# First attention batch: query scaling folded in, 64x64 turns, and work moved from VectorE to ScalarE and GpSimd

## The chip, the core and the metric

One core of a Trainium2 chip runs the whole program. Its engines are TensorE (PE, with its weight loads as PEld), VectorE (DVE), ScalarE (ACT), GpSimd (POOL) and SyncE (SP), which issues most of the DMA transfers; ScalarE's queue issues a few more at the start. The metric is the device time of one execution in microseconds, lower is better.

## The reference

A thresholded attention over 8 batches of 8 heads (576 rows, 64 columns a head), and then a bilinear feed-forward layer (FFN) over its 4608 x 512 output:

```python
scale = 1.0 / np.sqrt(q.shape[-1])
scores = scale * np.matmul(q, k.transpose(0, 1, 3, 2))
thresh = np.max(scores, axis=-1, keepdims=True) - tau
scores = np.where(scores >= thresh, scores, -1000000000.0)
scores = scores - np.max(scores, axis=-1, keepdims=True)
attn = np.exp(scores)
attn = attn / (np.sum(attn, axis=-1, keepdims=True) + 1e-09)
attn_out = np.matmul(attn, v)
# (B, H, S, D) -> x of (B*S, H*D)
a = x @ w_a
b = x @ w_b
return a * b @ w_out
```

The three weight matrices (512 x 1536 twice, 1536 x 512) arrive as 8-byte floats and are turned into 4-byte ones in the kernel, by operations on the integer halves.

## The kernel before

Two heads make a pair, four pairs (HP = 4) a batch. A *unit* (i, u) is 128 query rows of both heads of pair i. The first batch has 18 units, in the order (0,0), (1,0), (2,0), (3,0), (0,1), ... One pass of the main loop is a *slot* g: it works on several units at once, each at its own step. All instructions keep the order in which they are written, engine by engine (`keep_order`), so what stands ahead on an engine's queue runs first.

For its unit, slot g does:

- `scores` (L398 to L413): on TensorE the scores of both heads into two banks of the four in PSUM (L404); on VectorE each row's maximum (L411) and the threshold, maximum minus `cut` (L412).
- `weigh` (L423): on ScalarE, for each head, the bias (maximum times minus the scale, L431) and the exponential of scaled scores plus bias (L432); on VectorE the masked weights with their row sums (L435).
- `reciprocal` (L446, L448) on VectorE.
- For the first eight units (`BY_PE` = 8) `diagonals` (L456): ScalarE scales the identity by each head's reciprocals (L462). One slot later `turn_pe` (L469) transposes and normalises the weights in one: each of 9 column blocks of 64 is the stationary operand of a matmul with a head's diagonal (L479), 18 matmuls with 128 rows, 64 columns and 128 moving columns. ScalarE copies two banks of the result (L481), VectorE the ninth block (L482).
- Two slots later `weighted_unit` (L587) multiplies by the values (L542). `settle` (L546) copies the product out of PSUM: one half on ScalarE (L549), the other in two 64 x 64 pieces on VectorE (L550). GpSimd exchanges halves (L565).

Units from the ninth on are transposed by VectorE (L498) and by DMA through DRAM (`turn_blocks`, `turn_back`) instead.

Between these steps the weights are converted: 36 pieces of 0.5 MB, two or three a slot. A piece takes two passes on ScalarE (L298, L299), a clamp (L305) and an integer add (L324) on GpSimd, and two passes on VectorE (L311, L319). SP issues the loads of the pieces (L271); each is made to wait for the TensorE instruction that stands just before it in the program, and for the buffer that it fills. FFN matmuls of the first rows (L824, `pab`) start in slot 5, and fill TensorE between the attention steps. From about 130 us on TensorE goes through FFN and attention without a pause.

Ahead of the loop, ScalarE's queue issues the keys of pair 0 (L198) and then `tau` (L339); VectorE copies the transposed queries of pair 0 (L383) and then computes the scalars (L1042 to L1047): whether tau is at least 0, the scale and its negative, and `cut`.

Of the kernel before, what the change touches and what calls it, by code (L numbers as in the profile page):

```python
# [13 lines left out]
AF = mybir.ActivationFunctionType  # L14
ALU = mybir.AluOpType
AX = mybir.AxisListType
# [38 lines left out]
def kernel(  # L55
# [38 lines left out]
    nc = tc.nc  # L94
    B, H, S, D = q.shape
    P = 128
# [3 lines left out]
    HP = H // 2  # L100
    NT = 4
# [148 lines left out]
    first_sb = first_u32.bitcast(FP32)  # L250
# [77 lines left out]
    scalars = const.tile([P, 8], FP32, name="scalars")  # L328
    tau_sb = scalars[:, 5:6]
# [4 lines left out]
        rooms.append(t.rearrange("p n e -> p (n e)")[0:R, 0:ROWS])  # L334
    rooms += [sums_sb[0:R, c:c + ROWS] for c in range(0, 5 * ROWS, ROWS)]
    rooms = [t.rearrange("p (n w) -> p n w", n=NR) for t in rooms]
    load_rows(0, "q", rooms[0])
    load_rows(0, "k", rooms[1], nc.scalar)
    nc.scalar.dma_start(tau_sb, tau.to_broadcast([P, 1]))  # L339
    load_rows(1, "q", rooms[2])  # L340
    load_rows(1, "k", rooms[3], nc.scalar)
    load_weights(2)
# [5 lines left out]
    load_rows(3, "k", rooms[7])  # L348
    ident = more_sb[:, 2 * QUARTER:2 * QUARTER + P]
    make_identity(nc, ident)  # L350

# [4 lines left out]
    x_of, xtail_of = {}, {}  # L356
# [11 lines left out]
    def prep_pe(i, name):  # L368

        m = loaded[i][name]  # L370
        if name == "q":
            mT = first_sb[:, i * S:(i + 1) * S]
        else:
            mT = work.tile([P, S], FP32, tag="kT", bufs=HP, name="kT")
        tp = banks(SH, "tp")
        for c in range(2):
            for n in range(NR // 2):
                nc.tensor.transpose(tp[:, c, n * R:(n + 1) * R], m[:, c * (NR // 2) + n], ident[0:R, 0:R])
        prepared.setdefault(i, {})[name] = mT
        return mT, tp  # L380

    def prep_copy(mT, tp):
        nc.vector.tensor_copy(mT.rearrange("p (c k) -> p c k", c=2), tp)  # L383

    def columns():

# [2 lines left out]
    def scores(i, u):  # L389
        qT, kT = prepared[i]["q" if i < HP else "q1" if u > 1 else "q0"], prepared[i]["k"]  # L390
        base = HALF if i >= HP and u > 1 else 0
        sc = [banks(SH, "sc") for _ in range(2)]
        wide = D if u == NT else columns()
        each = [(c, t, j) for c in range(2) for t in range(2 if wide == D else 1) for j in range(2)]
        if units.index((i, u)) < BY_HEAD:
            each.sort(key=lambda x: x[2])
        for c, t, j in each:
            r = slice(j * D, (j + 1) * D)  # L398
            if u < NT:
                m, o, q0 = j, t, u * P + t * D - base  # L400
            else:
                m, o, q0 = t, j ^ t, MAIN - base
                qT, kT = prepared[i + t]["q" if i < HP else "q1"], prepared[i + t]["k"]
            nc.tensor.matmul(sc[m][o * D:o * D + wide, c], qT[r, q0:q0 + wide],  # L404
                             kT[r, c * SH:(c + 1) * SH], start=True, stop=True)
        mx = small.tile([P, 2], FP32, tag="mx", name="mx")
        thr = small.tile([P, 2], FP32, tag="thr", name="thr")
        bias = small.tile([P, 2], FP32, tag="bias", name="bias")
        for j in range(2):
            c = slice(j, j + 1)  # L410
            nc.vector.tensor_reduce(mx[:, c], sc[j], axis=AX.XY, op=ALU.max)  # L411
        nc.vector.tensor_scalar(thr, mx, cut, None, op0=ALU.subtract)  # L412
        scored[i, u] = (sc, thr, bias, mx)  # L413

    def rooms_of(i, u):
# [6 lines left out]
    def weigh(i, u):  # L422

        sc, thr, bias, mx = scored.pop((i, u))
        n = len(sc)
        sums = small.tile([P, 2], FP32, tag="sums", name="sums")
        ws = rooms_of(i, u)
        sb = [s.rearrange("p c (n e) -> p c n e", e=Q) for s in sc]
        wb = [w.rearrange("p (c n) e -> p c n e", c=2) for w in ws]
        for j in range(n):  # L430
            nc.scalar.activation(bias[:, j:j + 1], mx[:, j:j + 1], AF.Copy, scale=e_nscale)  # L431
            nc.scalar.activation(wb[j], sb[j], AF.Exp, bias=bias[:, j:j + 1], scale=e_scale)  # L432
# [23 lines left out]
    def diagonals(i, u):  # L456

        ws, rcp = weights[i, u]
        g = units.index((i, u))
        dg = first_sb[:, HP * S + g % 3 * 2 * P:HP * S + (g % 3 + 1) * 2 * P].rearrange("p (j q) -> p j q", j=2)  # L460
        for j in range(2):
            nc.scalar.activation(dg[:, j], ident, AF.Copy, scale=rcp[:, j:j + 1])  # L462
        weights[i, u] = (ws, dg)

    def turned_tile():
# [2 lines left out]
    def turn_pe(i, u):  # L468

        ws, dg = weights.pop((i, u))  # L470
        ws = [w.rearrange("p n e -> p (n e)") for w in ws]
        wT = turned_tile()[:, 0:G].rearrange("p g s e -> p (g s e)").rearrange("p (s w) -> p s w", w=P)
        turned[i, u, "pe"] = [wT[:, :, y * D:(y + 1) * D] for y in range(2)]
        tp = banks(512, "tp").rearrange("p y (s q) -> p y s q", s=NT)
        last = banks(P, "tp")
        for s in range(NSLOT):
            for j, w in enumerate(ws):
                to = (last[:, 0] if s == 2 * NT else tp[:, s // NT, s % NT])[j * D:(j + 1) * D]
                nc.tensor.matmul(to, w[:, s * D:(s + 1) * D], dg[:, j], start=True, stop=True)  # L479
        for y in range(2):  # L480
            nc.scalar.copy(wT[:, y * NT:(y + 1) * NT], tp[:, y])  # L481
        nc.vector.tensor_copy(wT[:, 2 * NT], last[:, 0])  # L482

    def parts(i, u):

# [57 lines left out]
                                     start=(s == 0), stop=(s == NSLOT - 1))  # L543
        return pv

    def settle(out, pv, c0, c1, others):  # L546

        n = c1 - c0
        one = [nc.scalar.copy(out[:, 0:n], pv[:, 0, c0:c1])]  # L549
        two = [nc.vector.tensor_copy(out[c * D:(c + 1) * D, n:2 * n], pv[(1 - c) * D:(2 - c) * D, 1, c0:c1])  # L550
               for c in range(2)]
# [38 lines left out]
    def weighted_unit(i, u):  # L590

        b, hp = pairs[i]
        wT = turned.pop((i, u, "pe"))
        pv = product([lambda rows, s, t=t: t[rows, s] for t in wT], loaded[i]["v"], P)
        settled_of[i] = settled_of.get(i, 0) + P
        if (b, 0) not in x_of:
            x_of[b, 0] = x_tile("xT")
            state["xs"] = x_tile("xS")
        settle(x_of[b, 0][:, hp, u * P:(u + 1) * P], pv, 0, D, ([], []))
        exchange(x_of[b, 0], state["xs"], hp, u * P, (u + 1) * P, nc.gpsimd)  # L600
        if hp == HP - 1:
# [436 lines left out]
    prep_copy(*prep_pe(0, "q"))  # L1038
    kT, tp = prep_pe(0, "k")
    nc.scalar.copy(kT.rearrange("p (c k) -> p c k", c=2), tp)  # L1040
    ok, e_scale, e_nscale, cut, big = (scalars[:, c:c + 1] for c in range(5))
    nc.vector.tensor_scalar(ok, tau_sb, 0.0, None, op0=ALU.is_ge)  # L1042
    nc.vector.tensor_scalar(e_scale, ok, SCALE, None, op0=ALU.mult)
    nc.vector.tensor_scalar(e_nscale, ok, -SCALE, None, op0=ALU.mult)
    nc.vector.tensor_scalar(big, ok, -BIG, BIG, op0=ALU.mult, op1=ALU.add)
    nc.vector.tensor_scalar(cut, tau_sb, 0.0, INV_SCALE, op0=ALU.max, op1=ALU.mult)
    nc.vector.tensor_tensor(cut, cut, big, op=ALU.add)  # L1047
    early = {}

    def convert_rest(g, k):  # L1050
# [6 lines left out]
    n = 0  # L1057
# [4 lines left out]
    for g in range(len(units) + PV_LAG):  # L1062
# [9 lines left out]
        if BY_PE + 1 < g <= len(units) + 1:  # L1072
            n = g - PV_LAG
# [3 lines left out]
        if here:  # L1077
            i, u = units[g]
# [9 lines left out]
            weighted_unit(*units[g - 2])  # L1088
            running["owed"] -= NSLOT * P // 2
        if g < 3:  # L1090
            prep_copy(*prep_pe(g + 1, "q"))
        convert_rest(g, 0)
        if g == 0:
            for c in range(0, 2 * QUARTER - 2 * CW + 1, 2 * CW):
# [131 lines left out]
```

## Time and profile before

| what | us |
|---|---|
| median of 3 timed runs | 1420.72 (1419.43 to 1420.96) |
| span of the profiled execution, first to last instruction | 1417.0 |
| TensorE busy in it | 1370.2 |
| VectorE / ScalarE / GpSimd busy | 1013.7 / 679.9 / 495.7 |
| TensorE idle before 130 us | 30.1 |
| VectorE busy between 76 and 110.3 us | 33.75 of 34.30 |
| TensorE idle from 130 to 1380 us | 10.3 |
| DMA rate, 24 to 76 us | 229 GB/s |

The profile is of one execution; its answers give that execution's span and no time from outside, so the table sets the span beside the timed runs: their median is 3.7 us more. "Busy" is the union of an engine's instructions; a line such as `PE 1370.2 (97%) x33836` gives busy time, its share of the span and the number of instructions. In the timeline a line gives start, duration, engine, source line, operation, output and input, shapes, a count, and in brackets the idle time of the engine before it with what ended it. "issue" there is a wait for nothing that the profile shows.

### The profile page before, as it was taken

How to read it: one execution, taken by the hardware profiler on the slowest of the kernel's cores; microseconds unless marked ns; L12 is line 12 of the kernel's file. 1: busy time of each engine (PE TensorE's matmuls, PEld its weight loads, DVE VectorE, ACT ScalarE, POOL GpSimd, SP SyncE). 2: the span in 40 equal slices, each digit the busy share in tenths (PEclk: the TensorE clock that was granted, in tenths of full speed). 3: DMA queues.
4: the chain of work that ended last, by engine and by line, in shares of the span. 5: the costliest groups of instructions: out<-in, count | busy, mean ns of one | idle time of the engine just before them, and what ended most of it. 6: DMA issues, size and time to landing. Idle time of an engine off the chain costs nothing.

```text
span 1417.0 us, 76257 instructions
## 1 busy us (share of the span) xinstructions
PE 1370.2 (97%) x33836; PEld 1229.6 (87%) x33836; DVE 1013.7 (72%) x2200; ACT 679.9 (48%) x1245; POOL 495.7 (35%) x678
## 2 busy tenths in 40 slices
PE   6788999999999999999999999999999999999998
PEld 5677579989878887979998999999888899799997
DVE  6898986778777877776767777677777776744424
ACT  5786554545445454545444545454545455431110
POOL 2674541606060606042333324150606060608100
PEclk9999999999999999999999999999999999999999
DMA  9967776667756775666555675567655775550000
GB/s 212 235 193 219 182 214 163 178 153 183 198 135 173 198 188 155 178 156 184 142 134 149 168 193 158 144 160 199 168 144 152 191 201 154 135 152 18 4 19 18
DMA packets 327000, 223.20 MB, mean 158 GB/s; under 512 B 171536, under 2 KB 310800, under 8 KB 326672
## 3 DMA queue, kind: packets, MB, share of 16 engines
q1 hardware_dynamic: 323712, 216.95, 59.2%
q8 instruction: 266, 4.36, 1.3%
q10 hardware_dynamic: 2960, 1.38, 0.4%
q14 instruction: 62, 0.51, 0.1%
HBM read 128.58 MB, written 89.65 MB: 154 GB/s over the span
## 4 chain that ended last, share of the span: by engine, by line
PE 86%; DVE 7%; DMA 3%; issue 2%; SPq 1%; ACT 0%; POOL 0%; DVEq 0%; POOLq 0%; ACTq 0%
PE pab L720 29%; PE po L885 20%; PE pab L824 16%; PE pv L542 10%; PE sc L404 10%; DVE mx L411 2%; DVE tw L498 2%; SPq L144 1%; DMA wT<-swap 1%; DVE tw L435 1%; PE tp L479 1%; DMA raw<-in_moe_w_a_dram 1%; DMA raw<-in_moe_w_b_dram 1%; DVE thr L412 0%; DVE u L790 0%
## 5 line engine op out<-in xcount | busy, mean ns | idle before, releaser
L411 DVE TENSOR_REDUCE mx<-sc 128x1 f32<-128x576 f32 x288 | 204.7, 752 | 125.8 <-PE sc L404 125.4
L454 ACT ACTIVATE tw<-tw,rcp 128x576 f32<-128x576 f32 x272 | 196.5, 770 | 202.3 <-DVE rcp L448 202.3
L682 POOL TENSOR_TENSOR h<-h,u 128x512 f32<-128x512 f32 x28 | 35.2, 1276 | 601.0 <-DVE h L794 426.1
L432 ACT ACTIVATE tw<-sc,bias,scalars 128x576 f32<-128x576 f32 x288 | 239.8, 833 | 10.9 <-PE pab L720 0.4
L435 DVE SCALAR_TENSOR_TENSOR tw<-sc,thr,tw 128x576 f32<-128x576 f32 x288 | 221.5, 799 | 10.4 <-ACT tw L432 9.9
L885 PE MATMUL po<-wo_sb,h 64*64 64x256 f32 x3264 | 205.8, 376 | 1.2 <-DVE h L794 1.1
L498 DVE STREAM_TRANSPOSE tw<-tw 128x576 f32<-128x576 f32 x272 | 194.4, 752 | 0.8 <-ACT tw L454 0.8
L885 PEld LDWEIGHTS po<-wo_sb,h 64*64 64x64 f32 x3264 | 157.0, 133 | 25.7 <-DVE h L794 2.6
L542 PE MATMUL pv<-wT,vm 64*64 64x160 f32 (+3 forms) x5184 | 169.2, 275 | 7.6 <-issue 3.6
L542 PEld LDWEIGHTS pv<-wT,vm 64*64 64x64 f32 x5184 | 157.4, 136 | 19.1 <-issue 9.8
L404 PE MATMUL sc<-kT,qT 64*64 64x288 f32 x2016 | 168.0, 404 | 1.1 <-DVE xt L550 0.5
L853 POOL TENSOR_TENSOR h<-h 128x256 f32<-128x256 f32 x168 | 117.4, 732 | 107.4 <-PE po L885 97.2
L885 PE MATMUL po<-sums_u,h 64*64 64x256 f32 x2448 | 153.4, 376 | 0.7 <-DVE h L832 0.7
L720 PE MATMUL pab<-xU,wb_sb 64*64 64x128 f32 x4352 | 138.0, 269 | 0.4 <-issue 0.3
L720 PEld LDWEIGHTS pab<-xU,wb_sb 64*64 64x64 f32 x4352 | 132.2, 133 | 3.7 <-issue 1.1
L885 PEld LDWEIGHTS po<-sums_u,h 64*64 64x64 f32 x2448 | 117.6, 133 | 19.4 <-DVE h L832 1.3
L404 PEld LDWEIGHTS sc<-kT,qT 64*64 64x64 f32 x2016 | 101.8, 133 | 22.6 <-issue 5.0
L549 ACT COPY xT<-pv 128x128 f32<-128x128 f32 (+1 forms) x68 | 17.7, 260 | 201.8 <-PE pv L542 200.2
L431 ACT ACTIVATE bias<-mx,scalars 128x1 f32<-128x1 f32 x288 | 83.1, 288 | 64.0 <-DVE mx L411 63.7
L550 DVE COPY xT<-pv 64x128 f32<-64x128 f32 (+1 forms) x136 | 38.1, 280 | 91.0 <-PE pv L542 89.7
L720 PE MATMUL pab<-xS,wa_sb 64*64 64x128 f32 x2176 | 101.8, 269 | 0.1
L531 ACT COPY kept<-po 128x512 f32<-128x512 f32 x65 | 34.8, 536 | 123.0 <-PE po L885 113.9
(156 smaller groups left out, 2414.3 us busy)
## 6 DMA issues: line engine op xcount, KB each, us to landing
wT<-swap SPq DMA_DIRECT2D x244, 288.0 KB, 3.9
swap<-tw SPq DMA_DIRECT2D x480, 144.0 KB, 2.9
vm<-in_v_dram SPq DMA_DIRECT2D x128, 72.0 KB, 2.5
swap<-tw SPq DMA_DIRECT2D x128, 72.0 KB, 3.0
kT<-in_k_dram SPq DMA_DIRECT2D x112, 72.0 KB, 3.3
wT<-swap SPq DMA_DIRECT2D x56, 144.0 KB, 3.3
out_dram<-kept SPq DMA_DIRECT2D x28, 256.0 KB, 3.9
qT<-in_q_dram SPq DMA_DIRECT2D x112, 40.0 KB, 2.8
```

The source lines that it names most:

```text
L404: nc.tensor.matmul(sc[m][o * D:o * D + wide, c], qT[r, q0:q0 + wide], kT[r, c * SH:(c + 1) * SH], start=True, stop=True)
L411: nc.vector.tensor_reduce(mx[:, c], sc[j], axis=AX.XY, op=ALU.max)
L431: nc.scalar.activation(bias[:, j:j + 1], mx[:, j:j + 1], AF.Copy, scale=e_nscale)
L432: nc.scalar.activation(wb[j], sb[j], AF.Exp, bias=bias[:, j:j + 1], scale=e_scale)
L435: nc.vector.scalar_tensor_tensor(out=wv, in0=sb[j], scalar=thr[:, j:j + 1], in1=wv, op0=ALU.is_ge, op1=ALU.mult, accum_out=sums[:, j:j + 1])
L454: nc.scalar.activation(w, w, AF.Copy, scale=rcp[:, j:j + 1])
L498: nc.vector.transpose(w, w)
L542: nc.tensor.matmul(pv[c * D:(c + 1) * D, y], vm[rows, s], wT[y](rows, s), start=(s == 0), stop=(s == NSLOT - 1))
L720: nc.tensor.matmul(out[c * D:(c + 1) * D, r, f * P:(f + 1) * P], w[g][k][rows, w0:w0 + D], moving[k][rows], start=(fresh and k == 0 and f ...
L824: nc.tensor.matmul(pab[c:c + columns(), r], w[rows, f // n, k, fs + c:fs + c + columns()], moving, start=(k == 0), stop=(k == H - 1))
L853: (nc.vector if state["over"] else nc.gpsimd).tensor_tensor(*a, **kw)
L885: nc.tensor.matmul(po[c * D:(c + 1) * D, r, y], ht[rows, t0:t0 + D], other[rows, f], start=(f == 0), stop=(f == NF // 2 - 1))
```

## The change

In the first batch (i < HP):

- the transposed queries are multiplied by the scale when they are copied out of PSUM (`prep_copy` with `e_scale`), so that the scores are scaled already; the scalars stand ahead of that copy, and the load of tau ahead of the keys of pair 0 on ScalarE's queue;
- the maxima are taken with their sign turned, and serve as the bias of the exponential; the bias instructions go;
- the threshold is taken on ScalarE, between the two exponentials: minus the negated maximum, plus a new scalar `ncut_first`.

In the first eight units:

- the diagonals are 64 columns for each row half (a 128 x 64 tile `twice`, two identities on top of each other, times the reciprocals), made by one GpSimd instruction for both heads;
- `turn_pe` does each block in four matmuls of 64 rows, 64 columns and 64 moving columns: 36 instead of 18;
- the ninth block and all of the product are copied by ScalarE.

```diff
+    nc.scalar.dma_start(tau_sb, tau.to_broadcast([P, 1]))
     load_rows(0, "q", rooms[0])
     load_rows(0, "k", rooms[1], nc.scalar)
-    nc.scalar.dma_start(tau_sb, tau.to_broadcast([P, 1]))
...
+    twice = first_sb[:, HP * S + 3 * P:HP * S + 3 * P + D]
+    nc.gpsimd.tensor_tensor(twice, ident[:, 0:D], ident[:, D:P], op=ALU.add)
...
+    def prep_copy(mT, tp, scale=None):
+        out = mT.rearrange("p (c k) -> p c k", c=2)
+        if scale is None:
+            nc.vector.tensor_copy(out, tp)
+        else:
+            nc.vector.tensor_scalar(out, tp, scale, None, op0=ALU.mult)
...
-            nc.vector.tensor_reduce(mx[:, c], sc[j], axis=AX.XY, op=ALU.max)
-        nc.vector.tensor_scalar(thr, mx, cut, None, op0=ALU.subtract)
+            nc.vector.tensor_reduce(mx[:, c], sc[j], axis=AX.XY, op=ALU.max, negate=i < HP)
+        if i >= HP:
+            nc.vector.tensor_scalar(thr, mx, cut, None, op0=ALU.subtract)
...
+            if i < HP:
+                nc.scalar.activation(wb[j], sb[j], AF.Exp, bias=mx[:, j:j + 1])
+                if j == 0:
+                    nc.scalar.activation(thr, mx, AF.Identity, bias=ncut_first, scale=-1.0)
+            else:
...
-        for j in range(2):
-            nc.scalar.activation(dg[:, j], ident, AF.Copy, scale=rcp[:, j:j + 1])
+        nc.gpsimd.tensor_tensor(dg, twice.unsqueeze(1).to_broadcast([P, 2, D]), rcp.unsqueeze(2).to_broadcast([P, 2, D]), op=ALU.mult)
...
         for s in range(NSLOT):
-            for j, w in enumerate(ws):
-                to = (last[:, 0] if s == 2 * NT else tp[:, s // NT, s % NT])[j * D:(j + 1) * D]
-                nc.tensor.matmul(to, w[:, s * D:(s + 1) * D], dg[:, j], start=True, stop=True)
-        for y in range(2):
-            nc.scalar.copy(wT[:, y * NT:(y + 1) * NT], tp[:, y])
-        nc.vector.tensor_copy(wT[:, 2 * NT], last[:, 0])
+            for r in range(2):
+                rows = slice(r * D, (r + 1) * D)
+                for j, w in enumerate(ws):
+                    to = (last[:, r] if s == 2 * NT else tp[:, r, s])[j * D:(j + 1) * D]
+                    nc.tensor.matmul(to, w[rows, s * D:(s + 1) * D], dg[rows, j], start=True, stop=True)
+        for r in range(2):
+            nc.scalar.copy(wT[:, 0:2 * NT, r * D:(r + 1) * D], tp[:, r])
+        nc.scalar.copy(wT[:, 2 * NT].rearrange("p (r q) -> p r q", r=2), last)
...
-        settle(x_of[b, 0][:, hp, u * P:(u + 1) * P], pv, 0, D, ([], []))
+        settle(x_of[b, 0][:, hp, u * P:(u + 1) * P], pv, 0, D, ([], []), nc.scalar.copy)
...
+    nc.vector.tensor_scalar(ncut_first, tau_sb, 0.0, -1.0, op0=ALU.max, op1=ALU.mult)
     nc.vector.tensor_tensor(cut, cut, big, op=ALU.add)
+    nc.vector.tensor_tensor(ncut_first, ncut_first, big, op=ALU.subtract)
+    prep_copy(*prep_pe(0, "q"), e_scale)
```

More of the change, by code (lines that the diff above doesn't have):

```diff
@@ L380, in prep_pe @@
         return mT, tp
-    def prep_copy(mT, tp):
-        nc.vector.tensor_copy(mT.rearrange("p (c k) -> p c k", c=2), tp)
+    def prep_copy(mT, tp, scale=None):
[4 more added lines that the diff above has]
+            nc.vector.tensor_scalar(out, tp, scale, None, op0=ALU.mult)
     def columns():
@@ L430, in weigh @@
         for j in range(n):
-            nc.scalar.activation(bias[:, j:j + 1], mx[:, j:j + 1], AF.Copy, scale=e_nscale)
-            nc.scalar.activation(wb[j], sb[j], AF.Exp, bias=bias[:, j:j + 1], scale=e_scale)
+            if i < HP:
[3 more added lines that the diff above has]
+            else:
+                nc.scalar.activation(bias[:, j:j + 1], mx[:, j:j + 1], AF.Copy, scale=e_nscale)
+                nc.scalar.activation(wb[j], sb[j], AF.Exp, bias=bias[:, j:j + 1], scale=e_scale)
         for j in range(n):
@@ L459, in diagonals @@
         g = units.index((i, u))
-        dg = first_sb[:, HP * S + g % 3 * 2 * P:HP * S + (g % 3 + 1) * 2 * P].rearrange("p (j q) -> p j q", j=2)
-        for j in range(2):
-            nc.scalar.activation(dg[:, j], ident, AF.Copy, scale=rcp[:, j:j + 1])
+        dg = first_sb[:, HP * S + g % 3 * P:HP * S + (g % 3 + 1) * P].rearrange("p (j q) -> p j q", j=2)
+        nc.gpsimd.tensor_tensor(dg, twice.unsqueeze(1).to_broadcast([P, 2, D]), rcp.unsqueeze(2).to_broadcast([P, 2, D]), op=ALU.mult)
         weights[i, u] = (ws, dg)
@@ L473, in turn_pe @@
         turned[i, u, "pe"] = [wT[:, :, y * D:(y + 1) * D] for y in range(2)]
-        tp = banks(512, "tp").rearrange("p y (s q) -> p y s q", s=NT)
-        last = banks(P, "tp")
+        tp = banks(512, "tp").rearrange("p y (s q) -> p y s q", q=D)
+        last = banks(D, "tp")
         for s in range(NSLOT):
-            for j, w in enumerate(ws):
-                to = (last[:, 0] if s == 2 * NT else tp[:, s // NT, s % NT])[j * D:(j + 1) * D]
-                nc.tensor.matmul(to, w[:, s * D:(s + 1) * D], dg[:, j], start=True, stop=True)
-        for y in range(2):
-            nc.scalar.copy(wT[:, y * NT:(y + 1) * NT], tp[:, y])
-        nc.vector.tensor_copy(wT[:, 2 * NT], last[:, 0])
+            for r in range(2):
[6 more added lines that the diff above has]
+        nc.scalar.copy(wT[:, 2 * NT].rearrange("p (r q) -> p r q", r=2), last)
     def parts(i, u):
@@ L544, in product, with settle @@
         return pv
-    def settle(out, pv, c0, c1, others):
+    def settle(out, pv, c0, c1, others, engine=None):
         n = c1 - c0
         one = [nc.scalar.copy(out[:, 0:n], pv[:, 0, c0:c1])]
-        two = [nc.vector.tensor_copy(out[c * D:(c + 1) * D, n:2 * n], pv[(1 - c) * D:(2 - c) * D, 1, c0:c1])
-               for c in range(2)]
+        copy = engine or nc.vector.tensor_copy
+        two = [copy(out[c * D:(c + 1) * D, n:2 * n], pv[(1 - c) * D:(2 - c) * D, 1, c0:c1]) for c in range(2)]
         for mine, theirs in ((one, others[1] + two), (two, others[0] + one)):
@@ L1036 @@
     second = {i: g for g, (i, u) in enumerate(units) if u == 2}
-    prep_copy(*prep_pe(0, "q"))
-    kT, tp = prep_pe(0, "k")
-    nc.scalar.copy(kT.rearrange("p (c k) -> p c k", c=2), tp)
     ok, e_scale, e_nscale, cut, big = (scalars[:, c:c + 1] for c in range(5))
+    ncut_first = scalars[:, 6:7]
     nc.vector.tensor_scalar(ok, tau_sb, 0.0, None, op0=ALU.is_ge)
@@ L1046 @@
     nc.vector.tensor_scalar(cut, tau_sb, 0.0, INV_SCALE, op0=ALU.max, op1=ALU.mult)
+    nc.vector.tensor_scalar(ncut_first, tau_sb, 0.0, -1.0, op0=ALU.max, op1=ALU.mult)
     nc.vector.tensor_tensor(cut, cut, big, op=ALU.add)
+    nc.vector.tensor_tensor(ncut_first, ncut_first, big, op=ALU.subtract)
+    prep_copy(*prep_pe(0, "q"), e_scale)
+    kT, tp = prep_pe(0, "k")
+    nc.scalar.copy(kT.rearrange("p (c k) -> p c k", c=2), tp)
     early = {}
@@ L1090 @@
         if g < 3:
-            prep_copy(*prep_pe(g + 1, "q"))
+            prep_copy(*prep_pe(g + 1, "q"), e_scale)
         convert_rest(g, 0)
```

## The prediction

> **What bounds the kernel now.** First the engine totals of the page, then a table of busy time by stage (columns: window in us, its length, then busy us and instruction count of TensorE, weight loads, VectorE, ScalarE and GpSimd, the granted clock, the DMA share, GB/s):
>
> ```profile
> PE 1370.2 (97%) x33836; PEld 1229.6 (87%) x33836; DVE 1013.7 (72%) x2200; ACT 679.9 (48%) x1245; POOL 495.7 (35%) x678
> ```
> ```profile
> 24.10:47.30 23.20, 18.45 (x384) 14.75 (x384) 21.82 (x53) 19.26 (x42) 14.19 (x19) 1.00 1.13 229
> 47.30:76.00 28.70, 23.76 (x457) 21.45 (x457) 23.60 (x53) 21.96 (x47) 20.14 (x24) 0.88 0.97 229
> 76.00:110.30 34.30, 27.56 (x514) 24.36 (x510) 33.75 (x66) 28.78 (x57) 24.97 (x27) 1.00 0.74 205
> ...
> 130.00:1380.00 1250.00, 1239.74 (x31316) 1114.13 (x31316) 889.12 (x1928) 584.46 (x1054) 423.78 (x591) 1.00 0.59 155
> ```
>
> From 130 us on TensorE is busy 1239.7 of 1250 us in an order that the change leaves alone. So the time changes by what the start-up before 130 us gains or loses, and that passes through whole. There are three stages in it. From 24 to 47 us VectorE is busy 94%, DMA is full. From 76 to 110 us VectorE is busy 33.75 of 34.30 us: it is the limit. Between them, from 47 to 76, no engine is, and the timeline shows why (start, us, engine, line, operation, count, idle before it):
>
> ```profile
> 33.20 1.28 PE L542 MATMUL pv<-wT,vm 64*64 64x64 f32 x72
> ...
> 34.41 2.19 PE L479 MATMUL tp<-first_u,tw 128*64 128x128 f32 x36
> ...
> 47.29 1.88 PE L542 MATMUL pv<-wT,vm 64*64 64x64 f32 x59 [0.56 <-issue]
> ...
> 54.66 1.16 PE L824 MATMUL pab<-xT,wb_sb 64*128 64x128 f32 x16 [0.56 <-issue]
> ...
> 62.58 0.54 PE L479 MATMUL tp<-first_u,tw 128*64 128x128 f32 x5 [1.13 <-issue]
> ...
> 70.09 0.34 PE L542 MATMUL pv<-wT,vm 64*64 64x64 f32 x6 [1.83 <-issue]
> ```
>
> TensorE stops four times in the middle of a run of like matmuls, waiting for no semaphore ("issue"). Counting its instructions in the trace (a weight load and a matmul each count one, a semaphore wait one), the holds stand before numbers 961, 1217, 1473 and 1729: 256 apart. The DMA view of a window between two of them names the cause:
>
> ```profile
> q1 hardware_dynamic: 196, 0.35, 101.0%
> q8 instruction: 1, 0.02, 5.1%
> issues: line engine op xcount, KB each, median us to landing
> more_u<-in_moe_w_b_dram SPq DMA_DIRECT2D x2, 256.0 KB, 8.8
> ```
>
> One 16,384-byte packet on the instruction queue at 51.86, among weight loads that fill the engines. Such packets start at 28.36, 36.25, 44.45, 51.86, 59.84, 67.31 and 71.96 us and take 1.3 us; each hold ends 1.46 to 1.57 us after one ends, and under full DMA the next starts 4.6 to 5.2 us after a hold ends. So I read it as code brought one block of 256 ahead, queued behind weight data: from 39.35 (entry to the block at 705) the blocks begin 7.94, 7.36, 7.93 and 7.51 us apart. TensorE gets 256 instructions per 7.7 us there, whatever the other engines do. At 70.09, with the queue nearly drained, the packet starts 1.87 us later: a cycle of 1.9+1.25+1.5 = 4.6 us.
>
> [...]
>
> **The change part by part.** g0, g1, ... are the slots (one unit each; scores of g0 at 8.1, g4 37.4, g5 44.4, g6 55.65, g7 65.8, g8 75.97, g9 85.0).
>
> *Removed from VectorE.* Rows of g8 and g9:
>
> ```profile
> 79.16 0.59 DVE L412 TENSOR_SCALAR thr<-mx,scalars 128x2 f32<-128x2 f32 x1
> ...
> 79.78 0.46 DVE L550 COPY xT<-pv 64x64 f32<-64x64 f32 x2
> ...
> 82.79 0.28 DVE L482 COPY wT<-tp 128x128 f32<-128x128 f32 x1
> ```
>
> Counted to the next start: threshold 0.17 to 0.64 (long when GpSimd runs beside it), the two product copies 0.49, the copy of the last block 0.2 to 0.28. The threshold goes in 18 units, the others in 8.
>
> *ScalarE.* Out: two biases (0.29 each, 36 in all) and two diagonals (0.70 the pair). In: a threshold (nearest rows: L444 128x2 0.20, L431 0.29), two 64x64 copies (L549 128x64 0.21, 0.11 when back to back), a 128x128 copy (0.26). Per early slot -1.28 against +0.9: nothing on the path. The masking pass now waits for a threshold behind the first exponential, 0.3 later on ScalarE than the old end of that exponential; but the bias before it (0.31) is gone, so equal. Behind the product copies stand the exponentials: +0.2, against the same bias.
>
> *GpSimd.* A 128x128 product per unit: between L853 (128x256, 0.73) and L682 (128x512, 1.28), extrapolated 0.46. It stands behind the clamp L305; in g4 that ends at 45.67, the reciprocals at 45.9, and the first reader ran at 49.1: covered by over 2 us. Bounds 0 to +0.5 a unit where the cover is gone. GpSimd is busy 20 of 28.7 us, so it still fits.
>
> *Start.* The tau load passes the key loads on ScalarE's queue: 0.53 later keys. TensorE's wait for them passed at 5.55 and it used them from 6.2: covered, 0 to +0.3. The scalars now stand ahead of the query copy: tau issued at 0.74, 4.5 to land, 0.7 of small operations: 5.9, before 6.46. The scaling copy: between 0.75 (L383) and 0.81 (L435), 4 times: at most +0.24. SP's queue keeps its order; only semaphores that tie it to the landings change.
>
> *TensorE.* Per unit 18 matmuls (36 records, 2.19 us) become 36 in the form of the products (72 records, 1.28): -0.91 us, but 72 instructions more. A slot with FFN work goes from 330 to 402 instructions in the built order.
>
> **The sum.** The block that ended at g2's scores (24.1) now ends inside the first turn, at about 20.2. Later block ends fall at the second turn's start, then at 67% of g3's products, 32% of g4's, in g5's scores, and 74% of g5's turn. Before, those points of the work were at 27.7, 34.1, 39.7, 46.0 and 51.3. At 7.6 us a block from 27.6 (20.2 and the 7.1 to 7.6 of a cycle) they come at 27.6, 35.2, 42.8, 50.4 and 58.0: **+6.7 us** by g5, and the VectorE savings of these slots lie beside the fetch, worth nothing. (Bounds: 7.1, the shortest cycle seen, +4.7; 7.94, +8.1.)
>
> What is late next: the weight loads. SP issues each behind an instruction of TensorE, and the waits view of the first 110 us has it waiting there already (us in total, times, longest):
>
> ```profile
> SPq L271 <- PE pab L824: 6.9, 3, 4.5
> ```
>
> The 20th weight piece stands behind g5's FFN matmuls, so it goes out near 63 instead of 56.3. The data queue drains by then, and the cycle should fall from 7.6 towards 4.6, at which 402 instructions take 7.2 us, less than a slot's matmuls. From that point of g5 to g8's scores before took 75.97-51.3 = 24.7. Off it: the holds 0.56+1.13+1.83 = 3.5; the half clock granted from 71.3 to 74.7 (turn 3.23 for 2.19, FFN 1.72 for 1.16), 1.6; 2.26 shorter turns, 2.05. On it: half clock after the long holds, 48 FFN matmuls at 1.72/16 for 1.16/16, +1.5; a rest of holds 0 to 3, taken as 1.2. That makes 20.3, g8 at 78.3: +2.3 (from -1 to +5).
>
> Then VectorE is the limit. It saves 0.62+0.49+0.28 in g8, 0.62+0.49 in g9, 0.17 in g10, 0.64 in g11: 3.3. After g12 some 0.5 of thresholds while VectorE is over 90% busy (150 to 170 us). Sum +2.3-3.3-0.5 = **-1.5 us**. The answers give the profiled execution its span alone, 1417.0; the median of the runs stands 3.7 above, which I keep: 1415.5+3.7 = **1419.2**.
>
> **Rivals.** *The holds don't grow (faster).* If code arrives in time, g2 to g5 gain what VectorE drops, 0.9 to 1.3 a slot, cut to about 2.7 where the weights of g4 and g5 land only 1 to 3.5 us before their use; g5 to g7 gain three turns, 2.7; g8 to g12 3.8: -9, 1411.5; with half of it 1415. For: the packet itself takes 1.3 us, and loads held back by TensorE shorten the queue. Against: four holds at exactly 256. [...]
>
> *The lateness is not made up (slower).* Code blocks in g6 to g8: if SP, freed in bursts of two or three 0.5 MB pieces, keeps the queue full, 1.57 blocks a slot at 6.5 us are 10.2 a slot, as now: 6.7 stays, less VectorE's 3.8, plus 0.5 of a late diagonal or keys: +3.5, 1424. It decides once the cycle in g6 and g7 exceeds about 5.5 us. For: 229 GB/s in that stage, close to the 244 of 110 to 130 us. Against: the 1.87 at 70.09.
>
> *It doesn't do what it says.* If four tiles take 2.2 us a unit (30 ns a record for 17.8), 2.7 of gain goes, +1.2: 1422.
>
> **Chances.** Forecast 0.42 (own range 1417 to 1421.5), faster rival 0.25, slower 0.25, last 0.08. No change means within 0.2% (2.8 us), about what a measurement of this kernel can tell. Faster by more: 0.25 and 0.08 of the forecast's, 0.33. Slower by more: 0.23 and 0.02 of the last, 0.25. Within: 0.42. Range 1413.5 to 1425.5: it leaves the better end of the first rival (0.1) and the worse of the second (0.08).
>
> **What would show it.** Holds of 2 to 5 us on "issue" between 32 and 58 us, before instruction numbers 256 apart; g6's scores near 63 instead of 55.65; shorter fetch cycles after 60; g8's near 78; the gap gone by 110. Turn rows of 72 records near 1.3 us. The forecast is wrong if g5's turn ends before 54, or if g9's scores are still over 4 us late.

## The result and the profile after

The changed kernel takes 1430.89 us (median of 5 runs, 1424.33 to 1433.06) against 1420.96 (5 runs, 1419.43 to 1421.72) on the same chip: a ratio of 1.0068, 95% interval 1.0041 to 1.0096. It is slower by some 9.7 us, where 1419.2 in a range up to 1425.5 was predicted. Its profiled execution took 1428.53 us, span 1426.7.

One caution for all that follows. The three times shown of the kernel before lay 1.5 us apart. 122 later runs of it lie between 1412.0 and 1433.5 us, mean 1420.5, standard deviation 3.7, so the interval above, from five runs of each, is likely too narrow. One trace is one draw, and below a mean over traces or runs stands wherever it can.

The stages of the changed kernel, in the windows that the prediction used (same columns: window, length, busy us and count of TensorE, weight loads, VectorE, ScalarE, GpSimd, granted clock, DMA share, GB/s):

```profile
24.10:47.30 23.20, 14.90 (x468) 12.24 (x468) 17.85 (x34) 14.67 (x35) 15.19 (x21) 0.93 1.13 228
47.30:76.00 28.70, 21.81 (x552) 18.88 (x552) 19.51 (x41) 20.40 (x48) 17.58 (x24) 0.82 0.85 210
76.00:110.30 34.30, 27.92 (x550) 25.43 (x552) 33.12 (x59) 27.54 (x58) 26.46 (x30) 0.95 0.70 199
130.00:1380.00 1250.00, 1233.76 (x31093) 1120.08 (x31097) 891.33 (x1932) 580.82 (x1049) 425.82 (x592) 1.00 0.59 156
```

In the first row every engine but GpSimd works less than before (VectorE 17.85 for 21.82, GpSimd 15.19 for 14.19) while DMA is as full: no engine's work is the limit. In the third VectorE is still at 33.12 of 34.30, although it has lost 16 operations between g6 and g12 (107 before, 91 now). In the last TensorE is busy 6 us less than before in the same 1250 us, though its order of work is the old one.

The timeline of TensorE (start, us, line, operation, count, idle before it and what ended it):

```profile
30.27 1.28 PE L492 MATMUL tp<-first_u,tw 64*64 64x64 f32 x72 [1.00 <-DVE first_u L389]
...
36.88 0.52 PE L555 MATMUL pv<-wT,vm 64*64 64x64 f32 x21 [1.05 <-issue]
...
44.21 0.97 PE L555 MATMUL pv<-wT,vm 64*64 64x64 f32 x49 [1.71 <-issue]
...
51.28 1.33 PE L410 MATMUL sc<-kT,first_u 64*128 64x288 f32 x2 [2.07 <-issue]
...
58.66 0.56 PE L492 MATMUL tp<-first_u,tw 64*64 64x64 f32 x19 [2.44 <-issue]
...
85.99 1.16 PE L837 MATMUL pab<-xT,wa_sb 64*128 64x128 f32 x16 [3.58 <-DVE tw L447]
90.34 1.28 PE L410 MATMUL sc<-kT,first_u 64*128 64x288 f32 x8
```

The holds on "issue" stand in front of TensorE's instructions 705, 961, 1217 and 1473, which resume at 36.9, 44.2, 51.3 and 58.7 us, 7.1 to 7.4 apart. Each resumes 1.35 to 1.56 us after the end of a 16,384-byte packet on the instruction queue (starts at 34.02, 41.37, 48.56 and 56.05 us, 1.26 to 1.30 long). So the first 63 us went as predicted. The line at 85.99 did not: after g8 TensorE waits 3.58 us for VectorE, and g9's scores (90.34) are 5.3 us late. In the kernel before the same matmuls waited 1.45 us:

```profile
82.27 1.16 PE L824 MATMUL pab<-xT,wa_sb 64*128 64x128 f32 x16 [1.45 <-DVE tw L435]
```

Matching TensorE's matmuls one by one, three traces of each kernel give this table. Start of the scores of a slot is in us; the last four columns are the delay of the same matmul against the first trace of the kernel before, at that trace's 160, 200 and 1390 us, and the sum of all holds over 0.15 us at block boundaries between 300 and 1390 us.

| trace | g6 | g8 | g12 | at 160 | at 200 | at 1390 | holds |
|---|---|---|---|---|---|---|---|
| before | 55.65 | 75.97 | 112.62 | 0 | 0 | 0 | 12.0 |
| before, again | 55.01 | 73.14 | 112.86 | 1.4 | 1.5 | 11.5 | 16.7 |
| before, third | 56.00 | 74.19 | 113.65 | -2.5 | -2.2 | 2.5 | 17.4 |
| changed | 63.56 | 78.85 | 118.29 | 1.2 | 4.2 | 9.2 | 18.7 |
| changed, again | 62.82 | 78.26 | 116.51 | 1.5 | 2.5 | 6.1 | 17.4 |
| changed, third | 62.85 | 78.14 | 115.93 | 2.7 | 5.8 | 12.7 | 20.4 |

In the means the changed kernel is 7.5 us late at g6, 4.0 at g8, 3.9 at g12, 2.2 at 160 us and 4.4 at 200. From 200 to 1390 it drifts 5.2 us, the kernel before 4.9. The last column is a rough measure: in the first trace of each kernel, such gaps around any other place in the blocks of 256 sum to 5 to 9 us as well, so only what lies above that belongs to the boundaries.

### The profile page after: what moved, and what is told of

The parts are those of the page before. It is cut to its first block, busy times and chain, and to the rows that moved or that the text cites. A ratio compares the mean times of both kernels' runs of the same rounds, so it can differ in the third digit from the quotient of the medians.

```text
span 1426.7 us, 76788 instructions
## 1 busy us (share of the span) xinstructions
PE 1368.2 (96%) x34124; PEld 1240.8 (87%) x34124; DVE 1006.7 (71%) x2160; ACT 669.4 (47%) x1235; POOL 500.8 (35%) x687
## 4 chain that ended last, share of the span: by engine, by line
PE 84%; DVE 9%; DMA 3%; issue 2%; SPq 1%; ACT 0%; ACTq 0%; POOL 0%; DVEq 0%; POOLq 0%
PE pab L733 28%; PE po L898 20%; PE pab L837 16%; PE sc L410 10%; PE pv L555 9%; DVE mx L417 2%; DVE tw L511 2%; DVE tw L447 1%; DMA wT<-swap 1%; DVE low L311 1%; SPq L144 1%; PE po L948 1%; DVE thr L419 0%; DMA swap<-tw 0%; DVE u L803 0%
## 5 line engine op out<-in xcount | busy, mean ns | idle before, releaser
L444 ACT ACTIVATE tw<-sc,bias,scalars 128x576 f32<-128x576 f32 x252 | 209.7, 832 | 9.6 <-PE po L898 0.4
L898 PEld LDWEIGHTS po<-wo_sb,h 64*64 64x64 f32 x3264 | 160.9, 133 | 22.3 <-DVE h L807 2.4
L898 PEld LDWEIGHTS po<-sums_u,h 64*64 64x64 f32 x2448 | 120.7, 133 | 16.9 <-DVE h L845 1.1
L443 ACT ACTIVATE bias<-mx,scalars 128x1 f32<-128x1 f32 x252 | 72.3, 287 | 64.3 <-DVE mx L417 64.0
L564 DVE COPY xT<-pv 64x128 f32<-64x128 f32 x120 | 34.6, 288 | 90.4 <-PE pv L555 89.4
```

The lines of the kernel that those rows point to most:

```text
L898: nc.tensor.matmul(po[c * D:(c + 1) * D, r, y], ht[rows, t0:t0 + D], other[rows, f], start=(f == 0), stop=(f == NF // 2 - 1))
```

## The experiments

There were eighteen further runs; five of them repeat a program, four of these for a second or third trace alone. A time is given as the ratio with its interval, and as the mean against the mean of the kernel before measured beside it (19 to 31 executions, standard error 0.6 to 0.9; the others have 5 to 12, with 0.8 to 1.4).

### One part alone

`turn_alone`: the kernel before, with `turn_pe`, `diagonals` and `twice` of the changed kernel.

> The kernel before with the four-tile turn of the first eight units alone (GpSimd's diagonals, last block copied by ScalarE); queries, maxima, thresholds, product copies and the tau load as before. 576 instructions more than before (64 over a multiple of 256). Theory 'fetch' (the first 130 us lose by the instructions of the turn, later by VectorE that can't catch up): holds at 705, 961, 1217, 1473 of 1 to 2.5 us as in the changed kernel, scores of g6 near 62.5, those of g9 4 to 6 us late, since VectorE has more to do than in the changed kernel, and in all +9 to +13 us, near 1432. Rival 'start and scalar work' (the loss comes from the tau load, the thresholds behind the exponentials and the scaled copies): scores of g9 less than 2 us late, and +5 or less in all (the phase's part alone).

`rest_alone`: the changed kernel, with the old two functions back and `nc.scalar.copy(wT[:, 2 * NT], last[:, 0])`.

> The changed kernel with the old turn (18 matmuls, ScalarE's diagonals; the last block is still copied by ScalarE): scaled queries, negated maxima, thresholds and product copies on ScalarE, tau loaded first. TensorE's instruction count is that of the kernel before. Theory 'turn' (the loss is the turn's, the rest saves VectorE 0.5 to 1.3 us a unit and pays some 1.4 us at the start): holds as in the kernel before, mean clock 0.995, 1417 to 1421. Rival 'start and scalar work': 1425 or more, with the clock near 0.989.

`extra72`, on the kernel before:

```
             to = (last[:, 0] if s == 2 * NT else tp[:, s // NT, s % NT])[j * D:(j + 1) * D]
+            nc.tensor.matmul(to[:, 0:32], w[:, s * D:(s + 1) * D], dg[:, j, 0:32], start=True, stop=True)
             nc.tensor.matmul(to, w[:, s * D:(s + 1) * D], dg[:, j], start=True, stop=True)
```

> The kernel before with its own turn of the first eight units, in which each of the 18 matmuls is preceded by one of 32 columns whose result is overwritten: 72 TensorE instructions more per unit, as many as the four-tile turn has more, and some 0.6 us more TensorE time per unit. Theory 'count' (the instructions themselves do it: code blocks queued behind weight data, then windows of half clock after the holds): holds in front of numbers 705, 961, 1217 and 1473 of 1 to 2.5 us, half-clock windows of 20 us or more before 180 us (13.65 in the kernel before), mean clock near 0.989, time near 1428, as with the four-tile turn alone, or up to 3 us more. Rival 'form' (four small tiles at once, GpSimd's diagonals or ScalarE's copies of the turn do it): holds and clock as before, 1421 to 1424.

| run | ratio | mean difference | mean clock | g6 |
|---|---|---|---|---|
| turn_alone | 1.0045 (1.0023 to 1.0067) | +6.8 us | 0.988 | 62.4 |
| rest_alone | 0.9996 (0.9974 to 1.0018) | -0.6 us | 0.995 | 55.4 |
| extra72 | 1.0036 (1.0014 to 1.0057) | +6.1 us | 0.995 | 63.2 |

The loss belongs to the turn; the rest is worth about nothing in time. With the old form of the turn and as many instructions, g6 is late by the same 7 to 8 us, and this hold stands where the turn in slot g5 crosses number 1473 (timeline of `extra72`):

```profile
57.81 0.32 PE L480 MATMUL tp<-first_u,tw 128*64 128x128 f32 x1 [2.50 <-issue]
...
63.22 1.24 PE L404 MATMUL sc<-kT,first_u 64*128 64x288 f32 x8
```

`extra72` alone would not part the count from TensorE's time, since its turn also takes longer (3.3 us for 2.19). `turn_alone` does: its turn is 0.91 us shorter than the old one, and g6 is late all the same. What the two have in common is the count of instructions, so it is this that makes g6 late, not the four tiles. One expectation failed: the clock of `extra72` is that of the kernel before. Of these three runs only `turn_alone` loses clock; TensorE is busy for 37.3 of its first 60 us, 43.2 in `extra72`.

### The tau load and the start

`rest_late` is `rest_alone`, and `after_late` the changed kernel, with this edit (the scaled copy now stands ahead of the scalars):

```
-    nc.scalar.dma_start(tau_sb, tau.to_broadcast([P, 1]))
     load_rows(0, "q", rooms[0])
     load_rows(0, "k", rooms[1], nc.scalar)
+    nc.scalar.dma_start(tau_sb, tau.to_broadcast([P, 1]))
...
+    prep_copy(*prep_pe(0, "q"), SCALE)
...
-                nc.scalar.activation(wb[j], sb[j], AF.Exp, bias=mx[:, j:j + 1])
+                nc.scalar.activation(wb[j], sb[j], AF.Exp, bias=mx[:, j:j + 1], scale=ok)
```

> The same with the tau load back behind the first keys, the query copies scaled by a constant (nothing waits for tau any more), and tau's sign applied in the exponential (for a tau of zero or more the same values). Theory 'tau first costs 1.4 us': first scores at 8.1 instead of 9.5 us, time 1.0 to 1.5 us below the run without this edit, 1415.5 to 1419.5. Rival: the start is covered by the later VectorE limit, the same time within 0.5 us.

> The changed kernel with the same late tau load and constant scale. Theory 'tau first costs 1.4 us': first scores near 8.1, 1429 or 1.0 to 1.5 us below the changed kernel. Rival 'fetch takes it all': the first block boundaries come 1.4 us earlier but the holds are set by the code queue behind weight data, so the scores of g6 stay near 63.5 and the time within 0.5 us of the changed kernel (1430).

First scores: 8.30 and 8.23 us, against 9.65 and 9.54. The tau load, with the copy that waits for it, did cost 1.3 us there. Times: `rest_late` 0.9983 (0.9959 to 1.0007), -2.8 us; `after_late` 1.0050 (1.0031 to 1.0070), +7.4 us, g6 at 62.46 for a mean of 63.08. In `after_late` the hold before number 1473 ends at 56.62 us for 58.66, so the code fetch did not take the gain; but the clock is at half from 48.5 to 62.2 us, and by g6 0.6 us of it is left, no more than traces of one program differ there (62.82 to 63.56). Neither expectation is met in full, and the times cannot tell 7.4 from the 9.7 of the changed kernel.

`rest_late_again` is the same program:

> The old turn with scaled queries, negated maxima, ScalarE's thresholds and copies and the late tau load once more, timed in more rounds: is it faster than the kernel before? Expected 2 to 3 us below (ratio 0.998, interval below 1), and a trace with g6's scores near 54.5 and 13 to 16 us of half clock. If the first measurement was chance, within 1 us of the kernel before.

0.9989 (0.9966 to 1.0011), -1.6 us. Both measurements point below the kernel before and neither excludes no change. No version that beats both kernels is shown.

### What the stage from g8 to g12 is limited by

`clamp_twice`, on `rest_late`:

```
-            nc.gpsimd.tensor_scalar(top, top, float_of(0x47EFFFFF), float_of(0x38000000),
-                                    op0=ALU.min, op1=ALU.max)
+            for _ in range(2 if 6 <= state["slot"] < 12 else 1):
+                nc.gpsimd.tensor_scalar(top, top, float_of(0x47EFFFFF), float_of(0x38000000),
+                                        op0=ALU.min, op1=ALU.max)
```

> The run with the old turn and the late tau load, in which GpSimd clamps every weight piece of slots g6 to g11 twice (the second changes nothing): some 13 operations of 128x512 more, 0.8 us each, 10 us of GpSimd, which has 14 of 54.7 us idle from g6's scores to g12's. Theory 'pair' (the weight conversions keep VectorE and GpSimd in each other's way, so that this stage takes 54 to 57 us whatever leaves VectorE): VectorE's shift, alone 0.42 us, goes from 0.83 to 1.0 or more on average, the stage from 54.7 to 58 to 62 us, time +3 to +7, near 1420 to 1423. Rival 'VectorE alone': VectorE's busy time and the stage within 1 us, time 1416.

The stage from g8's to g12's scores, in the same columns as above, first for the kernel before, then the changed kernel, then `clamp_twice`:

```profile
75.97:112.62 36.65, 29.91 (x552) 26.71 (x549) 35.80 (x71) 29.46 (x59) 25.22 (x27) 1.00 0.76 214
```
```profile
78.85:118.29 39.44, 31.67 (x588) 28.99 (x585) 37.11 (x66) 29.99 (x63) 28.79 (x30) 0.91 0.72 208
```
```profile
69.80:112.13 42.33, 32.93 (x552) 29.92 (x549) 38.91 (x65) 31.52 (x65) 38.52 (x43) 0.92 0.69 197
```

From g8 to g12 the three traces of the kernel before take 36.7, 39.7 and 39.5 us (mean 38.6), those of the changed kernel 39.4, 38.3 and 37.8 (38.5). `turn_alone`, which drops only the block copy from VectorE, takes 38.7. Operations leave VectorE, and the stage hardly gets shorter. More traces bear on it: `b32`, `b64` and `b128` below are the kernel before, and `a192` the changed kernel, up to 124 us. With them the mean is 39.3 in six traces of the kernel before and 38.3 in four of the changed one; the four with the old turn and the rest of the change (`rest_alone`, `rest_late` twice, `rest_late_64`) take 37.7.

From g6 to g12 the gain is plainer: 57.5 us in the six traces (55.8 to 59.4), 53.7 in the four of the changed kernel (53.1 to 54.7), 54.0 in the four with the old turn (53.0 to 54.7). The four traces with more instructions and nearly all of VectorE's old work (`turn_alone`, `extra72`, `turn_early`, `turn_late`) take 55.3. So lighter VectorE work alone saves 3.6 us here, and lateness alone is made up by 2.2, but the changed kernel, which has both, saves 3.9: on these traces the two do not add up.

What VectorE does in the place of the operations removed is seen in its shift of the weights (line groups of the windows from g8 to g12: operation, count, busy us, mean ns; kernel before, changed, `clamp_twice`):

```profile
L319 DVE TENSOR_SCALAR wa_sb<-wa_sb 128x512 uint32<-128x512 uint32 x4 | 2.9, 714 | 0.0
```
```profile
L319 DVE TENSOR_SCALAR wa_sb<-wa_sb 128x512 uint32<-128x512 uint32 x4 | 3.6, 896 | 0.0
```
```profile
L320 DVE TENSOR_SCALAR wa_sb<-wa_sb 128x512 uint32<-128x512 uint32 x4 | 4.0, 997 | 0.0
```

The same operation takes 714, 896 and 997 ns. This group changes most. Over all VectorE operations of the conversion in this stage (23 to 25) the mean is 0.74 to 0.77 us in the six traces of the kernel before, 0.82 to 0.84 in the four of the changed one, 0.83 to 0.84 in the four with the old turn and 0.95 in `clamp_twice`. Over 24 to 165 us of the changed kernel, the 14 shifts that meet no GpSimd operation average 0.42 us, the 6 beside one for nine tenths of their time 0.83. With 10.4 us more of GpSimd work (38.52 for the 28.12 of `rest_late` in this stage) the stage goes from 39.2 to 42.3 us, the time to 1.0009 (0.9982 to 1.0036), +2.0 us: 4.8 and 3.6 us above the two measurements of `rest_late`. The stage from g6 to g12 came out at 57.9 us (54.23 to 112.13) for the expected 58 to 62, and the conversions at 0.95 for 1.0 or more: both just short. The theory of the pair stands in the main: VectorE's busy time there includes time lost beside GpSimd (0.83 us a shift for 0.42 alone; with the clamps doubled, 0.95 us a conversion in the mean for 0.83 to 0.84). From g8 to g12, 3.0 us of other work leave VectorE in the changed kernel (23.3 to 20.3), and 24 conversions longer by 0.07 to 0.08 us give back some 1.8 of it. That all of it comes back is not shown. Nor does `clamp_twice` rule out that GpSimd, busy for 38.5 of its 42.3 us, had become a limit of its own.

### The place of the block boundaries

`b32`, `b64`, `b128` are the kernel before with 8, 16, 32 small matmuls in TensorE's idle time near 124 us, `a192` the changed kernel with 48, `rest_late_64` the run `rest_late` with 16:

```
         pv = banks(n // 2, "pv")
+        for z in range(extra_work):
+            j, c = z % 2, z // 2 % 2
+            rows = slice(j * D, j * D + D)
+            nc.tensor.matmul(pv[c * D:(c + 1) * D, j ^ c], ident[rows, rows], ident[rows, j * D:j * D + n // 2], start=True, stop=True)
```

> The kernel before with 16 small matmuls (64 TensorE instructions, results overwritten by the product that follows) put in front of the first tail product, near 124 us, where TensorE has idle time: from there on every block of 256 instructions begins 64 instructions earlier in the work, which is the phase that the changed kernel has (575 instructions more in all, 63 over a multiple of 256). Theory 'phase' (the steady part of the changed kernel is slower because its block boundaries fall at other places): +5 to +8 us, near 1427. Rival 'the changed work itself' (the steady part is slower for another reason, for instance later starts of its loads): +0 to +1 us, near 1421.

> The same with 32 small matmuls, 128 instructions: a third phase. Theory 'phase': another time than before and than the run with 64, somewhere in -3 to +10 us; the boundary holds between 300 and 1390 us (before 11.97 us in 47 gaps over 0.15 us, changed kernel 18.69 in 59) sum to something else again. Rival: +0 to +1 us and about 12 us of holds.

> The changed kernel with 48 small matmuls (192 instructions) at the same place: 767 more than before in all, so that the boundaries fall within one instruction of where the kernel before has them. Theory 'phase': the 5.5 us that the changed kernel loses between 300 and 1390 us come back, and most of the 2.9 at 170 us: 1430.9 - 5.5 to 8.4 = 1422.5 to 1425.4. Rival: 1431, the holds of the steady part stay near 18.7 us.

> The kernel before with 8 small matmuls (32 TensorE instructions) near 124 us: the block boundaries from there on as in the runs that have the four-tile turn in one half of the units, and nothing else changed. Theory 'phase' (where the boundaries fall in the part that is full of TensorE work costs some 3 us by itself; the 64 and 128 instructions cost 2.3 and 4.0 in the mean): a hold of 1.8 to 2.1 us at 166 to 168 us, holds between 300 and 1390 us of 15 to 18 us (12.0, 16.7 and 17.4 in three traces of the kernel before), mean time +2.5 to +4, so that half a turn by itself costs about 1. Rival 'the turn itself': +0 to +1, and half a turn costs the 4 us measured.

> The run with the old turn and the late tau load (mean 2.8 and 1.6 us below the kernel before in two measurements) with 16 small matmuls near 124 us: 64 instructions, the phase of the changed kernel. Theory 'phase': its gain goes, +0 to +2 us against the kernel before, 2.5 to 4 above the run without them, with a hold of 1.2 to 2.4 us at 160 to 168 us. Rival 'the place does not matter': still 1.5 to 3 us below the kernel before.

| run | ratio | mean difference | holds 158 to 180 us | holds 300 to 1390 |
|---|---|---|---|---|
| b32 | 1.0001 (0.9980 to 1.0021) | +0.3 us | 1.4 | 15.2 |
| b64 | 1.0017 (0.9996 to 1.0037) | +2.3 us | 3.0 | 13.7 |
| b128 | 1.0034 (1.0014 to 1.0054) | +4.0 us | 0.4 | 18.5 |
| a192 | 1.0044 (1.0020 to 1.0069) | +5.9 us | 1.0 | 16.7 |
| rest_late_64 | 0.9997 (0.9979 to 1.0014) | +0.1 us | 2.1 | 14.8 |

One part of the theory is shown. All eight traces with some 64 instructions more hold 1.3 to 3.3 us between 158 and 180 us; eight traces with the old place (the kernel before three times, the four with the old turn, and `a192`) hold 0.5 to 1.0. Between 160 and 200 us the first eight fall back by some 2.2 us in the mean, the other eight by 0.4. The hold cuts the same tail product in `b64`, where nothing else is changed, as in the changed kernel (timeline, `b64` first):

```profile
169.52 0.48 PE L546 MATMUL pv<-wT,vm 64*64 64x32 f32 x18 [1.22 <-issue]
```
```profile
171.58 0.47 PE L555 MATMUL pv<-wT,vm 64*64 64x32 f32 x17 [1.64 <-issue]
```

The other part, 5.5 us in the steady part by the place, is not. `b32` costs nothing although it has 15.2 us of holds, `b64` is within 0.4% of the kernel before, `a192` wins back 3.8 of the 9.7 us at most, and `rest_late_64` against `rest_late` (-2.8 and -1.6) is some 2 us, hardly more than its error. Only `b128` is slower by an interval that leaves out no change; its trace falls back by 3.6 us between 160 and 200 us although its boundary holds there are short, and why is open. The second and third traces of the kernel before settle most of it:

> The kernel before once more, for a second trace of it. If the changed kernel's loss of 5.6 us between 200 and 1390 us is its own, this trace follows the first one there: holds at block boundaries between 300 and 1390 us near 12 us, no drift over 2 us against the first trace. If it is chance from execution to execution, drift and holds differ by 3 us or more between the two traces of one program.

> The kernel before a third time, for its trace: its two traces differ by 10.0 us of drift between 200 and 1390 us, and by 1.5 at 200. If the steady part is chance from execution to execution, this drift (against the first trace) lies anywhere from 0 to 10 us; the time at 200 us within 2 us of the first.

> The changed kernel once more, for a second trace. Its own properties should come back: holds before 705, 961, 1217 and 1473, scores of g6 near 63 and a wait of TensorE for VectorE after g8, a hold of over 1.5 us at 167 to 172 us, 24 us or more of half clock before 180 us. The holds between 300 and 1390 us: near 18.7 if the drift belongs to the program, 12 to 17 if it is chance.

> The changed kernel a third time: at 200 us it stood 4.2 and 2.5 us behind the first trace of the kernel before, and drifted 5.1 and 3.6 us from there to 1390. If the change costs in the start alone, 2 to 5 us behind at 200, and a drift within those of the kernel before (0 to 10).

The unchanged program drifted 10.0 and 4.7 us against its own first trace between 200 and 1390 us, with 16.7 and 17.4 us of holds for 12.0. The first trace was a low draw there. Steady-part TensorE time of it and of the second trace (200 to 1390 us):

```profile
200.00:1390.00 1190.00, 1181.13 (x30559) 1077.47 (x30555) 832.49 (x1803) 543.62 (x977) 383.38 (x560) 1.00 0.58 152
```
```profile
200.00:1390.00 1190.00, 1175.77 (x30167) 1077.41 (x30162) 826.62 (x1797) 544.00 (x978) 384.11 (x561) 1.00 0.58 152
```

5.4 us less TensorE work fits into the same 1190 us of one and the same program. The 5.0 us that the first pair of traces shows after 200 us is therefore no finding about the change.

### Half of the turn

`turn_early` and `turn_late` are the kernel before with `turn_pe` and `diagonals` of the changed kernel where `units.index((i, u)) < 4`, or `>= 4`, and the old ones elsewhere.

> The kernel before with the four-tile turn in units g0 to g3 alone (turned in slots g1 to g4, which run before 50 us, where weight data fill the DMA engines); the other four keep the old turn. 288 TensorE instructions more (32 over a multiple of 256). Theory 'code behind weight data' (instructions cost where the weights fill the DMA engines): g6's scores near 60 to 63, +4 to +7 us, near 1425 to 1428. Rival 'every four-tile turn costs alike': half of the whole turn's cost, +3.4, and the same as with the other four.

> The kernel before with the four-tile turn in units g4 to g7 alone (turned in slots g5 to g8, from about 50 us on); the first four keep the old turn. The same 288 instructions more, so the same place of the block boundaries from 80 us on. Theory 'code behind weight data': holds before 45 us as in the kernel before, g6's scores at 55 to 58, 0 to +2 us, 1420 to 1423. Rival 'every four-tile turn costs alike': +3.4, near 1424, no difference to the run with the first four.

1.0033 (1.0012 to 1.0054), +4.3 us, and 1.0030 (1.0009 to 1.0051), +3.8 us. The expectation that only the early turns cost is wrong: each half costs about half. In the traces g6 is late by 1.2 us (56.78) and 2.5 us (58.05), where scores at 60 to 63 were expected of the early ones. In `turn_late` the hold falls into the first four-tile turn (timeline):

```profile
47.23 1.11 PE L510 MATMUL tp<-first_u,tw 64*64 64x64 f32 x64
49.70 0.33 PE L510 MATMUL tp<-first_u,tw 64*64 64x64 f32 x4 [1.35 <-DVE xT L584]
52.48 0.48 PE L510 MATMUL tp<-first_u,tw 64*64 64x64 f32 x4 [2.45 <-issue]
```

The hold on "issue" is no tax of the first four turns alone; the late ones have it too (2.45 us here), and in these traces the whole turn's 7.5 us at g6 is more than the two halves' 3.7 together. Why the halves cost 4 us in the mean of runs when their single traces stand 2.0 and 0.2 us late at 200 us is not settled by these runs.

## Why the prediction was wrong

**What bounds the kernel** held: four holds 256 instructions apart, code behind weight data (a 16,384-byte packet on the instruction queue ends 1.35 to 1.56 us before each hold does, at a DMA share of 1.11 from 24 to 60 us), a cycle of 7.1 to 7.4 us for the 7.6 taken.

**The four-tile turn** held: 72 records in 1.28 us. The rival that it would not run at that speed is out.

**The sum up to g8** held against the trace it was made from: holds at the four places named, g6 at 63.56 for 63, the 20th weight piece issued at 63.77 for 63, g8 at 78.85 for 78.3. Against the mean of three traces g8 is 4.0 us late instead of 2.9, because the first trace of the kernel before had a half-clock window at 71.3 to 74.7 us that its other two did not have.

**The start** was mis-sized: "covered, 0 to +0.3" for keys 0.53 us later. TensorE waited 0.83 us for the keys, and first scores came 1.4 us late. Little of that reaches g6 (0.6 us by `after_late`).

**"Then VectorE is the limit. It saves ... 3.3" is the step that failed.** From g8 to g12 the stage got 0.1 us shorter by three traces of each kernel, 0.9 by six and four. The prediction read 33.75 busy of 34.30 as 33.75 us of work. Part of it was time lost beside GpSimd: 3.0 us of operations did leave VectorE, but the conversions went from 0.76 to 0.83 us each and gave back some 1.8. `clamp_twice` shows the same from the other side. The prediction also added this saving to a catching-up of TensorE of 4.4 us (6.7 to 2.3) by g8, as if the two were independent. The conversions of these slots were still to be done, hence the 3.58 us wait: 7.7 us were to be made up by g12, and 3.6 were (7.5 to 3.9). The runs that have only one of the two make up 2.2 and 3.6. With this step at 0.1 to 0.9 the forecast's own sum is some 2.4 to 3.2 us higher: 1421.6 to 1422.4.

**"So the time changes by what the start-up before 130 us gains or loses, and that passes through whole" failed too.** The order of TensorE's work is unchanged, but 575 instructions more move every later block boundary by 63. Between 160 and 200 us the three traces of the changed kernel lose 2.2 us more than those of the kernel before, by the hold at 170 us and, in two of the three, a half-clock window right behind it; `b64` has the hold without any other change.

**The sum now.** By the traces the changed kernel is 2.2 us late at 160 us and 4.4 at 200, where the forecast had it 1.0 to 1.5 us early. At their ends the three traces of each kernel lie 4.8 us apart in the mean. The times lie further apart: 9.7 us in the first comparison, 6 to 7 put together from other runs (turn +6.8 and rest -0.6; `after_late` +7.4), and 9.0 between the mean of all seven executions of the changed kernel (1429.5) and that of the 122 of the kernel before. Three traces of each kernel are too few: those of the kernel before are of executions some 3 us slower than its mean, those of the changed one of executions 1 us faster. Where the other executions lose the remaining 2 to 5 us is open. Of the 3.7 us that the forecast kept between span and median, some 1.8 is there in each execution that has both times; the rest was the draw of the first trace.

The same holds for gains. The three traces of the old turn with the late tau load stand 5.7 to 6.8 us ahead of the kernel before at 200 us, and the mean times of these runs (`rest_late` twice, `rest_late_64`) 2.8 and 1.6 below and 0.1 above it; each trace is of an execution 3 to 5 us faster than the mean of its run. That a gain in the start passes through whole is therefore not shown either.

**The rivals.** The slower one, lateness not made up, gave 1424 and had the right sign, at another place: it looked for it in code blocks of g6 to g8, and g6 to g8 did make up 3.5 us. The faster one is out.

## What to carry to other kernels

An engine that is 98% busy (VectorE with 33.75 of 34.30 us) is not yet 98% at work: before counting a saving on it, compare the same operation alone and beside its neighbour (here 0.42 and 0.83 us), and do not add it to another saving in the same stage. Here, where a 16,384-byte packet of instructions came before each hold while data filled the DMA engines (share 1.11 from 24 to 60 us), an edit that makes work shorter by using more instructions (0.91 us less a turn, 72 instructions more) was priced by its instructions (g6 7.5 us late), and it moved every later block boundary (by 63). And three close times are no measure of scatter: take a second trace of the unchanged kernel before explaining a drift.

## What the runs showed of the hardware beyond that

The granted clock falls to half in windows of 3.41 us. In the first trace of each kernel every stretch at half clock before 200 us is one or two of them long (3.41 or 6.83 us), and within a trace the starts lie whole multiples of 3.413 us apart: 47.43, 71.32 and 125.93 us before (7 and 16 windows), 25.61, 49.50, 59.74, 87.05, 114.35 and 172.38 in the changed kernel (7, 3, 8, 8 and 17). Between the two traces they do not: 47.43 and 49.50 are 2.07 us apart. Around two of the changed kernel's windows (columns as above; the clock is the third figure from the end):

```profile
46.10:49.50 3.40, 1.65 (x15) 0.94 (x10) 2.58 (x8) 3.40 (x8) 2.01 (x4) 1.00 1.07 268
49.50:56.33 6.83, 4.93 (x127) 3.99 (x127) 3.02 (x5) 3.93 (x11) 3.93 (x8) 0.50 1.07 259
56.33:59.74 3.41, 1.08 (x29) 1.02 (x31) 3.24 (x9) 1.25 (x4) 1.24 (x1) 1.00 1.05 267
59.74:63.15 3.41, 3.41 (x38) 3.41 (x36) 0.54 (x2) 2.46 (x7) 2.07 (x3) 0.50 0.46 129
```

Here a window with TensorE busy for 1.65 us of 3.40, or 1.08 of 3.41, is followed by half clock, and full clock comes back after a window that is busy nearly throughout (3.30 us in the second half of the second row, 3.41 in the last). A rule by the busy share does not come out of the traces: in the same trace windows with TensorE busy for 1.68 us (from 35.85) and 1.88 us (from 42.67) were followed by full clock, and in the kernel before one with 2.49 us (from 44.02) by half. The longest gap of TensorE between 24 and 60 us of the changed kernel is 2.44 us, shorter than one window.

All runs with the whole four-tile turn have a mean clock of 0.988 to 0.989, the kernel before 0.995: some 18 us more at half clock over 1420 us (2 x 0.0065 x 1420). In the three traces of each kernel most of this lies before 200 us (25.0 us at half clock for 12.5), where the delays above include it. `extra72`, slower by 6.1 us at 0.995, says that a loss of this size does not need it.
